# A new order of one instruction list: a state-space scan and a low-rank mixer on one core

## Chip, cores and metric

The kernel runs on one core of a Trainium2 chip. The metric is the device time of one execution in microseconds (us), median of the runs. The engines are TensorE (PE in the profile, PEld for its weight loads), VectorE (DVE), ScalarE (ACT), GpSimd (POOL) and SyncE (SP), whose queue issues all the loads and stores.

## What is computed

The first part is a chunked scan over 4 batches of 8 heads, 768 tokens, 32 channels and 16 states; the second mixes tokens through a rank of 32 and channels through two weight matrices.

```python
# scan: x (4,8,768,32), a (4,8,768), B and C (4,8,768,16); chunks of 32 tokens
cum = cumsum(log(a) in the chunk)
M = (C @ B.T) * exp(cum_i - cum_j) * causal
y = M @ x + (C @ state) * exp(cum)
state = exp(cum_last) * state + sum_j exp(cum_last - cum_j) * B_j x_j
# bridge: (b, h, s, d) -> x (4, 768, 256)
# mixer: U (768,32), V (32,768), w_ch1 (256,1024), w_ch2 (1024,256)
u = x + ((x.T @ U) @ V).T
out = u + relu(u @ w_ch1) @ w_ch2
```

U, V and the two matrices arrive as 64-bit floats. The kernel loads them as 32-bit words and makes fp32 of them itself.

## The kernel before

The scan is cut into 12 pairs of 128-token blocks, three for each batch: pairs 0 to 2 are batch 0, 3 to 5 batch 1, and so on. The mixer works on a batch in two halves of 384 tokens and on the hidden size in eight slices of 128. Batch 0 takes plain fp32 products for its channel mixing; the later batches split each operand into parts of fewer bits (near, far, and a joined one) and multiply those in a faster type.

Nothing is scheduled by the compiler. A string, PLAN, holds some 900 words, and `follow` runs through it, so each engine gets its instructions in the order of the words. A word is a letter and its indices. Each engine runs its own list in order and waits on semaphores for the others, so a word that waits on an engine holds back all the words behind it there. The letters that matter here:

- F n: n fill products are put ahead of the next product that takes a PSUM bank (`idle`, L139). Nobody reads them; one is two records in the profile.
- A 0, A 1: the decay products (L370, L374) and their Exp (L377). K: the decays between chunks (L385 to L397).
- Q k.c and P k: B and C of pair k times their decays, on VectorE (tile BC), in three parts or at once. V k.c.v and T k: transposes of BC (L475) and the copies of them (T, Cm).
- g k: C times B (L507, banks x and z). m k and M k: the causal mask over its first and second half, on VectorE (tile M). s k: what a pair adds to the state (L542), u k: the state itself (tile S on VectorE, Sm on GpSimd).
- n k, i k, j k: the outputs of pair k (L652, L627, L652), in two banks y. j waits for a tiny VectorE copy (tile `settled`) behind n and i. y k: their copies (L670). t k and O k.v: the transposes to token order (L679).
- c n: the next of three steps that make fp32 of a loaded chunk (the generator `to_fp32`): VectorE and ScalarE first, then VectorE, then GpSimd (L422). Chunk 0 is U and V together, 1 and 2 are the halves of the first quarter of w_ch1, 3 to 5 its other quarters, 6 to 9 are w_ch2. v: V spread and split (L838 to L848).
- R n: the next step that splits a converted chunk into its parts (`refine`: ScalarE, then GpSimd at L436, with ScalarE and VectorE).
- p b, q b: the projection by U (L705, L713). a b.j: u of half j (L723 on TensorE, adds on VectorE).
- U 0.j.m: the plain products of slice m for batch 0 (L751, tile w1f) and their Relu. S, f, e, h: the split of u and the first product of the later batches. d: the second product, in pieces, and the output.
- B k, X k, w n, L k: loads of pair k's B and C, of its x, of a weight chunk (w 0 and 1 are halves of 256 KB, the others 512 KB, and chunk number n + 1 is made of w n), and of both B and X. A load word in PLAN carries a wait for the last VectorE instruction ahead of it (`hold`).

All loads go through SP's queue, in order. In the kernel before, the first nine (LOADS: B0 X0 B1 V0 U0 X1 B2 X2 B3) stand ahead of the plan and wait for nothing.

All VectorE rows of the profile have line L169, that of a helper, so one goes by the tiles.

Of the kernel before, what the change touches and what calls it, by code (L numbers as in the profile page):

```python
# [10 lines left out]
FP32 = mybir.dt.float32  # L11
INT32 = mybir.dt.int32
UINT32 = mybir.dt.uint32
FP32R = mybir.dt.float32r
WCOLS = 512
NWORDS = 15
# [14 lines left out]

LOADS = (
    'B0 X0 B1 V0 U0 X1 B2 X2 B3 ')
PLAN = (
    'F5 A0 Q0.0 F1 F2 F4 w0 Q0.1 A1 Q0.2 V0.0.0 Q1.0 V0.1.1 K0 s0 Q1.2 g0 m0 Q1.1 M0 V1.0.2 '
    'V1.1.2 u0 n0 g1 c0 c0 c0 M1 F1 i0 Q2.0 s1 j0 y0 m1 Q2.2 Q2.1 V2.0.2 u1 V2.1.3 n1 i1 g2 j1 y1 '
    'B5 s2 m2 M2 w1 v0 u2 O0.0 w2 w3 c1 c1 c1 i2 P3 n2 j2 y2 t1 X3 T3 T3 B4 c2 c2 P5 O2.1 p0 g3 '
    'c3 c3 w4 w5 m3 q0 M3 T5 w6 T5 a0.1 a0.0 s3 X4 c4 c4 c2 P4 U0.1.0 c5 c3 U0.0.3 U0.0.0 U0.0.2 '  # L40
    'c4 c5 B6 X5 U0.1.1 T4 T4 U0.0.4 u3 n3 c6 i3 R2 g4 s4 j3 R1 M4 R0 c5 X6 m4 u4 U0.0.7 P6 c6 '
    'U0.1.7 w7 U0.0.5 w8 y3 U0.1.6 U0.1.4 R1 s5 n4 i4 c6 g5 c7 c7 c7 L8 u5 j4 y4 T6 T6 U0.0.1 M5 '
    'U0.0.6 m5 c9 n5 i5 R4 g6 c8 c8 j5 y5 t4 d0.1.0.0 t3 m6 t5 U0.1.5 c9 L7 c9 R7 U0.1.2 P8 p1 '
    'U0.1.3 M6 R5 P7 R3 q1 d0.1.0.1 c8 d0.1.0.2 d0.1.0.3 d0.0.1.0 a1.0 R0 S1.0 d0.0.2.0 d0.0.2.1 '
    'd0.0.2.2 d0.0.2.3 L10 T7 d0.0.1.1 d0.0.1.2 R3 T7 d0.0.1.3 n6 R2 R5 g7 m7 s6 f1.0.4 M7 a1.1 '
    'u6 f1.0.1 e1.0.4 h1.0.4 f1.0.0 f1.0.5 e1.0.1 e1.0.0 h1.0.0 d0.0.0.0 e1.0.5 d0.0.0.1 R4 L9 T8 '
    'f1.0.6 h1.0.5 f1.0.7 T8 e1.0.6 d0.0.0.2 h1.0.1 d0.0.0.3 e1.0.7 i6 s7 j6 f1.0.2 d0.1.2.0 R6 '
    'h1.0.6 h1.0.7 y6 f1.0.3 e1.0.2 h1.0.2 d0.1.2.1 u7 e1.0.3 h1.0.3 S1.1 P9 d0.1.2.2 d0.1.1.0 '
    'd0.1.2.3 d0.1.1.1 d0.1.1.2 d0.1.1.3 n7 R4 g8 m8 i7 M8 s8 d1.0.0.0 d1.0.0.1 R6 R7 R7 R6 R5 u8 '
    'f1.1.1 d1.0.0.2 L11 d1.0.0.3 d1.0.1.0 f1.1.0 s9 P10 j7 y7 d1.0.0.4 e1.1.0 u9 h1.1.0 d1.0.0.5 '  # L50
    'd1.0.1.1 e1.1.1 d1.0.1.2 d1.0.2.0 d1.0.2.1 h1.1.1 f1.1.6 d1.0.2.2 f1.1.7 d1.0.1.3 e1.1.6 T9 '
    'h1.1.6 T9 d1.0.1.4 d1.0.1.5 T10 d1.0.2.3 e1.1.7 t7 h1.1.7 f1.1.3 f1.1.2 d1.0.2.4 d1.0.2.5 '
    'e1.1.2 h1.1.2 T10 e1.1.3 f1.1.4 f1.1.5 n8 i8 s10 j8 e1.1.4 e1.1.5 y8 d1.1.0.0 h1.1.3 '
    'd1.1.1.0 d1.1.1.1 h1.1.4 P11 d1.1.0.1 h1.1.5 d1.1.2.0 d1.1.2.1 d1.1.0.2 d1.1.0.3 u10 '
    'd1.1.2.2 d1.1.2.3 d1.1.0.4 d1.1.0.5 d1.1.1.2 d1.1.1.3 d1.1.2.4 d1.1.2.5 d1.1.1.4 d1.1.1.5 t6 '
    't8 g9 m9 p2 T11 i9 M9 q2 T11 g10 m10 n9 M10 a2.0 s11 j9 u11 y9 g11 m11 S2.0 M11 i10 t9 n10 '
    'f2.0.0 f2.0.4 f2.0.5 e2.0.0 j10 h2.0.0 y10 e2.0.4 h2.0.4 f2.0.1 e2.0.5 h2.0.5 f2.0.2 e2.0.1 '
    'h2.0.1 f2.0.6 f2.0.3 e2.0.2 e2.0.6 f2.0.7 h2.0.2 e2.0.3 h2.0.6 i11 n11 j11 h2.0.3 e2.0.7 '
    'd2.0.0.0 h2.0.7 d2.0.1.0 d2.0.1.1 y11 a2.1 S2.1 d2.0.0.1 d2.0.0.2 d2.0.0.3 d2.0.1.2 d2.0.1.3 '
    't10 t11 d2.0.1.4 d2.0.1.5 d2.0.0.4 d2.0.0.5 f2.1.1 f2.1.0 f2.1.2 f2.1.3 e2.1.0 h2.1.0 e2.1.1 '  # L60
    'h2.1.1 p3 e2.1.2 d2.0.2.0 h2.1.2 d2.0.2.1 d2.0.2.2 q3 f2.1.4 e2.1.3 h2.1.3 d2.0.2.3 f2.1.5 '
    'e2.1.4 d2.0.2.4 d2.0.2.5 e2.1.5 f2.1.7 h2.1.4 h2.1.5 f2.1.6 d2.1.2.0 a3.0 e2.1.6 e2.1.7 '
    'd2.1.0.0 h2.1.6 a3.1 d2.1.0.1 d2.1.0.2 d2.1.2.1 d2.1.2.2 S3.0 f3.0.2 f3.0.3 f3.0.4 h2.1.7 '
    'd2.1.0.3 d2.1.2.3 e3.0.2 f3.0.7 h3.0.2 e3.0.3 d2.1.0.4 d2.1.0.5 e3.0.4 f3.0.6 d2.1.1.0 '
    'd2.1.1.1 d2.1.1.2 f3.0.5 h3.0.3 e3.0.6 d2.1.2.4 e3.0.7 h3.0.4 e3.0.5 h3.0.6 h3.0.7 f3.0.0 '
    'd2.1.1.3 h3.0.5 f3.0.1 d2.1.2.5 e3.0.0 e3.0.1 d2.1.1.4 h3.0.0 d2.1.1.5 S3.1 d3.0.2.0 '
    'd3.0.2.1 d3.0.0.0 h3.0.1 d3.0.0.1 f3.1.2 f3.1.3 d3.0.2.2 d3.0.2.3 f3.1.5 f3.1.0 d3.0.2.4 '
    'd3.0.2.5 e3.1.2 h3.1.2 e3.1.3 h3.1.3 d3.0.0.2 d3.0.0.3 d3.0.1.0 f3.1.4 d3.0.1.1 f3.1.1 '
    'e3.1.4 h3.1.4 e3.1.5 h3.1.5 e3.1.0 e3.1.1 h3.1.0 d3.0.1.2 d3.0.1.3 h3.1.1 d3.0.0.4 f3.1.6 '
    'f3.1.7 d3.0.1.4 e3.1.6 d3.0.1.5 e3.1.7 d3.0.0.5 d3.1.2.0 d3.1.2.1 h3.1.6 h3.1.7 d3.1.2.2 '  # L70
    'd3.1.2.3 d3.1.1.0 d3.1.1.1 d3.1.2.4 d3.1.2.5 d3.1.1.2 d3.1.1.3 d3.1.0.0 d3.1.0.1 d3.1.0.2 '
    'd3.1.0.3 d3.1.1.4 d3.1.1.5 d3.1.0.4 d3.1.0.5 ')


@with_exitstack
def kernel(
# [28 lines left out]
    P = 128  # L105
    NB, NH, S, D = x.shape
    N = B.shape[-1]
    NC = S // P
    NPR = NC // 2
    DM = NH * D  # L110
    RK = moe_U.shape[1]
# [6 lines left out]
    NQ = NM // 2  # L118
# [75 lines left out]
    def begin(**kwargs):  # L194
        op = nc.sync.dma_start(**kwargs)
        if until:
            hold(op, until.pop())

    def load_bc(k, blocks=(0, 1)):
        b, q = pairs[k]  # L200
        if k not in bc_sb:
            bc_sb[k] = raw.tile([P, NH, 2, 2, N], FP32, tag="bc", name="bc")
        for c in blocks:
            begin(
                out=bc_sb[k][:, :, 0, c],
                in_=B[b, :, ts(2 * q + c, P), :].rearrange("h s n -> s h n"))
            if c == 0:
                begin(
                    out=bc_sb[k][:, :, 1].rearrange("p h t n -> p h (t n)"),
                    in_=C[b, :, ts(q, 2 * P), :].rearrange("h (p t) n -> p h (t n)", t=2))  # L210
# [17 lines left out]
    w1all = mix.tile([P, NQ, NCB, W], FP32, tag="u", name="w1f", bufs=1)  # L228
    w1f = [w1all[:, c] for c in range(NQ)]
    w2 = [const.tile([P, NM, DM], FP32R, name=f"w2{i}") for i in range(2)]  # L230
    weights = []
    w2f, w2b = {}, {}

    def w2c(n, dtype):
        return (w2f if dtype == FP32 else w2b).setdefault(n, mix.tile(
            [P, 2, DM], dtype, tag=f"w2c{n}", name=f"w2c{n}", bufs=1))


    def words_of(dst):
        p, i, j = dst.shape  # L240
        t = raw.tile([P, 2 * WCOLS], INT32, tag="words", name="words", bufs=NWORDS)
        weights.append((dst, t[:p, :2 * i * j]))
        return t[:p, :2 * i * j]

    def each(parts, *index):
        return [part[index] for part in parts]

    def load_words(dst, src):

        p, i, j = dst.shape  # L250
        t = words_of(dst)
        begin(out=t.rearrange("p (i j) -> p i j", i=i), in_=src)

    U2, V2, w12, w22 = (w.bitcast(INT32) for w in (moe_U, moe_V, moe_w_ch1, moe_w_ch2))
# [3 lines left out]
    own = {}  # L258

    def load_v():  # L260
        own["UV"] = words_of(UV)
        for q in range(4):
            begin(out=own["UV"][ts(q, Q), 2 * NC * RK:], in_=V2[:, ts(q, 2 * NC * RK)])

    def load_u():
        begin(out=own["UV"][:, :2 * NC * RK].rearrange("p (c r) -> p c r", c=NC),
                          in_=U2.rearrange("(c p) r -> p c r", p=P))

    def load_w(n):
        if n < 2:  # L270
            if n == 0:
                own["w"] = words_of(w1f[0])
                weights.pop()
            dst, t = w1f[0][:, :, ts(n, P)], own["w"][:, ts(n, 2 * NCB * P)]
            weights.append((dst, t))
            begin(out=t.rearrange("p (i j) -> p i j", i=NCB),
                  in_=w13[:, :, ts(n, 2 * P)])
        elif n <= NQ:
            load_words(w1f[n - 1], w13[:, :, ts(n - 1, 2 * quarter)])
        else:  # L280
            m = 2 * (n - NQ - 1)
            load_words(w2c(n - NQ - 1, FP32), w22[m * P:(m + 2) * P].rearrange(
                "(m p) d -> p m d", p=P))

    def load(k):
        if k < NB * NPR:
            load_bc(k)
            load_x(k)

    loads = dict(B=load_bc, X=load_x, w=load_w)  # L290
    for word in LOADS.split():
        dict(loads, V=lambda n: load_v(), U=lambda n: load_u())[word[0]](int(word[1:]))

    ident = const.tile([P, P], FP32)
    make_identity(nc, ident)
# [578 lines left out]
    def ytokens_of(k, v):  # L874
# [1 line left out]

    scans = dict(P=prep, T=turned, g=gram, s=state, m=lambda k: mask(k, (0, 1)),
                 M=lambda k: mask(k, (2, 3)), u=update, i=inter, n=lambda k: intra(k, 0),
                 j=crossed, y=yout, t=ytokens, L=load, Q=lambda k, c: prep(k, c, 1),
                 O=ytokens_of,  # L880
                 V=lambda k, c, v: turn(k, c, 1, "wx"[v // 2], vector if v % 2 else None))
    whole = dict(c=convert, R=refined, A=lambda i: decays(every_batch, "w", [i]),
# [3 lines left out]
    def follow(plan):  # L886

        for word in plan.split():
            name, at = word[0], [int(v) for v in word[1:].split(".")]
            if name in "BXwL":  # L890
                until[:] = [vector.last]
            if name in loads:
                loads[name](*at)
            elif name in scans:
                scans[name](*at)
            elif name in whole:
                whole[name](*at)
            else:
                b, *at = at
                if b not in mx:  # L900
                    mx[b] = mixer(b)
                getattr(mx[b], name)(*at)
            until.clear()
# [32 lines left out]
```

## Time and profile before

| | before |
|---|---|
| median of 3 runs | 230.32 us (229.53 to 230.38) |
| the profiled execution | 229.32 us |
| its span | 227.6 us |
| TensorE busy, records | 215.0 us (94%), 3004 |
| VectorE busy, instructions | 146.5 us (64%), 312 |
| ScalarE busy, instructions | 107.9 us (47%), 250 |
| GpSimd busy, instructions | 33.9 us (15%), 43 |
| moved by DMA | 14.56 MB in 69,518 packets, 63,792 of them under 512 B |
| packets that carry instructions | 23 of queue q8 (0.38 MB), 7 of q14 |

An engine's busy time is the sum over its instructions. A matmul's end is modelled, since products overlap in the array, so TensorE busy is not TensorE at its peak. The chain of waits runs back from the last instruction to what released each step; its pieces are given as start, length, engine, tile and line. "issue" is time in which an engine waited for nothing that the profile shows. Windows are stretches of the span, with each engine's busy time and instruction count in them, the granted TensorE clock (PEclk, 1.00 is full), the share of the DMA engines and GB/s.

### The profile page before, as it was taken

The numbers are of one execution on the slowest core, as the hardware profiler recorded it, in microseconds if no ns is written. First come the engines' busy times: TensorE is split into PE (matmuls) and PEld (weight loads), VectorE is DVE, ScalarE is ACT, GpSimd is POOL, SyncE is SP. The second block draws the span as 40 slices with busy tenths as digits, with TensorE's granted clock in tenths as the row PEclk, the third lists the DMA queues.
The fourth block names the chain that finished last, engine by engine and source line by source line (L and its number), as shares of the span: only waits on it lengthen the run. The fifth ranks groups of instructions, "written<-read, shape, count | busy, mean of one in ns | idle before, by whom it ended". The sixth has DMA issues, their size and how long they took to land.

```text
span 227.6 us, 6973 instructions
## 1 busy us (share of the span) xinstructions
PE 215.0 (94%) x3004; PEld 183.3 (81%) x3004; DVE 146.5 (64%) x312; ACT 107.9 (47%) x250; POOL 33.9 (15%) x43
## 2 busy tenths in 40 slices
PE   7867979999999999999999999999999999999993
PEld 5644636666658889887999897698999999999993
DVE  4597867678632686479746546967746964945731
ACT  2334643756854366532456511465445654636410
POOL 3031232335075003015200010000000000000000
PEclk9999988999999999999999999999999999999999
DMA  6896878976560164211430001000010000000011
GB/s 95 137 130 111 154 180 162 232 106 202 80 94 23 35 106 49 42 32 50 53 65 27 22 27 49 3 3 0 3 46 3 24 0 26 23 23 26 23 46 46
DMA packets 69518, 14.56 MB, mean 64 GB/s; under 512 B 63792, under 2 KB 67696, under 8 KB 69488
## 3 DMA queue, kind: packets, MB, share of 16 engines
q1 hardware_dynamic: 69488, 14.13, 31.5%
q8 instruction: 23, 0.38, 0.6%
q14 instruction: 7, 0.06, 0.1%
HBM read 10.98 MB, written 3.15 MB: 62 GB/s over the span
## 4 chain that ended last, share of the span: by engine, by line
PE 82%; DVE 10%; issue 2%; ACT 2%; POOL 1%; POOLq 0%; DVEq 0%
PE x L751 29%; PE z L751 20%; PE y L751 12%; PE y L652 3%; PE y L627 3%; DVE M L169 3%; PE x L507 2%; PE w L679 2%; DVE words L169 2%; PE w L705 2%; DVE S L169 2%; PE w L475 2%; DVE BC L169 2%; PE w L542 1%; PE w L139 1%
## 5 line engine op out<-in xcount | busy, mean ns | idle before, releaser
L751 PE MATMUL x<-u,w 128*128 128x384 f32 x144 | 33.3, 345 | 0.1
L751 PE MATMUL z<-u,w 128*128 128x384 f32 x144 | 33.0, 344 | 0.0
L169 DVE SCALAR_TENSOR_TENSOR words<-words 128x768 fp32r<-128x768 f32 (+3 forms) x34 | 29.7, 873 | 2.1 <-PE y L751 0.4
L751 PEld LDWEIGHTS x<-u,w 128*128 128x128 f32 x144 | 24.5, 188 | 1.1 <-ACT words L785 0.4
L751 PEld LDWEIGHTS z<-u,w 128*128 128x128 f32 x144 | 24.8, 188 | 0.3
L169 DVE SCALAR_TENSOR_TENSOR words<-x,words 128x384 fp32r<-128x384 f32 x24 | 13.2, 555 | 17.7 <-ACT words L785 17.5
L756 ACT ACTIVATE x<-x 128x384 f32<-128x384 f32 (+1 forms) x30 | 13.7, 455 | 21.8 <-PE x L751 19.6
L751 PE MATMUL x<-w2c,words 128*128 128x256 f32 x112 | 22.4, 338 | 0.0
L756 ACT ACTIVATE z<-z 128x384 f32<-128x384 f32 (+1 forms) x27 | 12.5, 464 | 15.3 <-PE z L751 14.4
L569 POOL TENSOR_TENSOR Sm<-S,own 128x256 f32<-128x256 f32 (+1 forms) x12 | 7.7, 640 | 78.6 <-DVE S L169 60.1
L751 PEld LDWEIGHTS x<-w2c,words 128*128 128x128 f32 x112 | 18.3, 189 | 1.4
L751 PE MATMUL y<-w,words 128*128 128x256 f32 x144 | 19.3, 282 | 0.0
L751 PEld LDWEIGHTS y<-w,words 128*128 128x128 f32 x144 | 18.6, 190 | 0.0
L169 DVE SCALAR_TENSOR_TENSOR words<-z,words 128x384 fp32r<-128x384 f32 x24 | 13.2, 552 | 2.6 <-ACT words L785 2.6
L785 ACT ACTIVATE words<-x 128x384 fp32r<-128x384 f32 x24 | 11.7, 493 | 6.8 <-PE x L751 6.8
L785 ACT ACTIVATE words<-z 128x384 fp32r<-128x384 f32 x24 | 11.7, 491 | 6.7 <-PE z L751 6.7
L169 DVE TENSOR_TENSOR BC<-bc,F 128x512 f32<-128x512 f32 (+2 forms) x18 | 10.4, 594 | 5.5 <-ACT F L377 2.8
L507 PE MATMUL x<-Cm,T 32*64 32x128 f32 x192 | 11.0, 306 | 2.5 <-issue 1.4
L652 PE MATMUL y<-M,x 64*32 64x64 f32 x768 | 12.0, 223 | 1.5 <-DVE settled L169 1.5
L751 PE MATMUL x<-w,words 128*128 128x256 f32 x96 | 13.4, 284 | 0.0
L652 PEld LDWEIGHTS y<-M,x 64*32 64x32 f32 x768 | 8.2, 105 | 6.0 <-DVE settled L169 2.7
L751 PEld LDWEIGHTS x<-w,words 128*128 128x128 f32 x96 | 12.6, 190 | 0.1
(148 smaller groups left out, 406.4 us busy)
## 6 DMA issues: line engine op xcount, KB each, us to landing
words<-in_moe_w_ch_dram SPq DMA_DIRECT2D x7, 512.0 KB, 5.6
x<-in_x_dram SPq DMA_DIRECT2D x24, 128.0 KB, 3.4
out_dram<-ytok SPq DMA_DIRECT2D x24, 128.0 KB, 1.7
bc<-in_B_dram SPq DMA_DIRECT2D x24, 64.0 KB, 3.0
bc<-in_C_dram SPq DMA_DIRECT2D x12, 128.0 KB, 3.1
words<-in_moe_w_ch_dram SPq DMA_DIRECT2D x2, 256.0 KB, 3.2
words<-in_moe_V_dram SPq DMA_DIRECT2D x4, 48.0 KB, 2.0
words<-in_moe_U_dram SPq DMA_DIRECT2D x1, 192.0 KB, 3.0
```

Source lines behind the costliest of these rows:

```text
L139: nc.tensor.matmul(out=t[:, :m * w].rearrange("p (m i) -> p m i", i=w), lhsT=ident, rhs=ident[:, None, :w].to_broadcast([P, m, w]), start= ...
L169: self.last = call(*args, **kwargs)
L475: nc.tensor.transpose(out=tp[:, i, v], in_=s["BC"][:, i, c + v].rearrange("p h n -> p (h n)"), identity=ident)
L507: nc.tensor.matmul(out=g[r][cols, c], lhsT=s["T"][rows, 0, c, cols], rhs=s["Cm"][rows, :, :, ts(2 * c + p, Q)].rearrange("r v t i -> r v i ...
L569: nc.gpsimd.tensor_tensor(out=s["Sm"][:, sl], in0=s["S"][:, sl].rearrange("p i (s d) -> p i s d", s=2), in1=own2[:, b, 4 * q + sl.start:4 ...
L627: behind["first"].append(nc.tensor.matmul(out=y[r // 2][ts(r % 2, H), c, p], lhsT=own[ts(r, Q)], rhs=s["T"][ts(r, Q), 1, :, ts(2 * c + p, ...
L652: product = nc.tensor.matmul(out=y[n][ts(i, Q), c, p], lhsT=x_sb[k][half, c, h], rhs=s["M"][half, h // 2, c, h % 2], start=fresh(k, n, [i] ...
L679: nc.tensor.transpose(out=t[:, c, g], in_=yT[b][:, g, ts(2 * q + c, P)], identity=ident)
L705: nc.tensor.matmul(out=p[ts(c % 4, Q)], lhsT=U_sb[:, c], rhs=ytok[b][:, c], start=c < 4, stop=True, skip_group_check=True)
L751: nc.tensor.matmul(out=t, lhsT=lhsT, rhs=rhs, start=start, stop=True, skip_group_check=True)
L756: nc.scalar.activation(t, t, AF.Copy, scale=1.0 + EPS)
L785: nc.scalar.activation(gs[j, m // 2][0][:, m % 2], t, AF.Relu, scale=NEAR)
```

## The change

The operations stay as they are. PLAN is replaced by another order of the same words, from its first word to its last, and the load words are mixed into it:

- F5 and the last of F1 F2 F4 ahead of A0 and A1, and an F1 later (ten fills), become F2 ahead of A0 and F2 ahead of V0.0.0 (four fills).
- The first nine loads become words with a Y ahead of their letter (YB0, YX1, YV0). They wait for nothing, as before. Their order is now B0 B1 X0 X1 V0 B2 U0, then w1, which waits, then X2 and B3: V and U come behind the second x.
- The three steps of c0 go from behind g1 to places among the words of pairs 1 and 2, right ahead of v0.
- The chunks of w_ch1 are loaded in the order w1 w2 w0 w4 w3 w5 instead of w0 w1 w2 w3 w4 w5, and converted in an order to match, with the first steps of c2 and c3 between the words of pairs 2 and 3 and c1 behind a0 and a1. The U products start with slices 3, 2, 1, 0 instead of 0, 3, 0, 2.
- n3 goes ahead of the first U. The later scans, splits and products have another order too.
- L goes; B and X are separate words for all pairs.

The head of the plan, before and after (the rest of the list is left out; it is reordered in the same way):

```diff
-LOADS = (
-    'B0 X0 B1 V0 U0 X1 B2 X2 B3 ')
 PLAN = (
-    'F5 A0 Q0.0 F1 F2 F4 w0 Q0.1 A1 Q0.2 V0.0.0 Q1.0 V0.1.1 K0 s0 Q1.2 g0 m0 Q1.1 M0 V1.0.2 '
-    'V1.1.2 u0 n0 g1 c0 c0 c0 M1 F1 i0 Q2.0 s1 j0 y0 m1 Q2.2 Q2.1 V2.0.2 u1 V2.1.3 n1 i1 g2 j1 y1 '
-    'B5 s2 m2 M2 w1 v0 u2 O0.0 w2 w3 c1 c1 c1 i2 P3 n2 j2 y2 t1 X3 T3 T3 B4 c2 c2 P5 O2.1 p0 g3 '
-    'c3 c3 w4 w5 m3 q0 M3 T5 w6 T5 a0.1 a0.0 s3 X4 c4 c4 c2 P4 U0.1.0 c5 c3 U0.0.3 U0.0.0 U0.0.2 '
-    'c4 c5 B6 X5 U0.1.1 T4 T4 U0.0.4 u3 n3 c6 i3 R2 g4 s4 j3 R1 M4 R0 c5 X6 m4 u4 U0.0.7 P6 c6 '
-    'U0.1.7 w7 U0.0.5 w8 y3 U0.1.6 U0.1.4 R1 s5 n4 i4 c6 g5 c7 c7 c7 L8 u5 j4 y4 T6 T6 U0.0.1 M5 '
-    'U0.0.6 m5 c9 n5 i5 R4 g6 c8 c8 j5 y5 t4 d0.1.0.0 t3 m6 t5 U0.1.5 c9 L7 c9 R7 U0.1.2 P8 p1 '
-    'U0.1.3 M6 R5 P7 R3 q1 d0.1.0.1 c8 d0.1.0.2 d0.1.0.3 d0.0.1.0 a1.0 R0 S1.0 d0.0.2.0 d0.0.2.1 '
+    'YB0 F2 A0 Q0.0 A1 YB1 Q0.1 F2 Q0.2 V0.0.0 Q1.0 YX0 V0.1.1 K0 g0 Q1.2 m0 Q1.1 M0 s0 V1.0.2 '
+    'V1.1.2 YX1 YV0 n0 g1 u0 i0 YB2 Q2.0 s1 m1 YU0 j0 y0 w1 Q2.2 M1 Q2.1 YX2 n1 u1 V2.0.2 V2.1.3 c0 '
+    'i1 YB3 g2 c0 B5 w2 j1 X3 M2 w0 B4 y1 s2 m2 c0 v0 O0.0 t1 u2 i2 n2 c2 j2 y2 P3 T3 T3 P5 O2.1 c3 '
+    'w4 c3 p0 c3 g3 m3 q0 T5 T5 M3 a0.0 c2 a0.1 c1 n3 w3 s3 U0.0.3 U0.0.2 X4 c2 P4 U0.0.1 T4 T4 w5 '
+    'c1 c1 U0.1.0 u3 i3 U0.1.1 c5 c5 X5 w7 j3 y3 c4 c4 R0 g4 c4 s4 m4 M4 B6 w8 w6 X8 U0.1.2 U0.0.0 '
+    'u4 i4 g5 n4 s5 j4 m5 c5 R3 B7 U0.0.4 U0.0.5 B8 X6 B11 y4 M5 R0 c6 X10 u5 U0.1.4 t3 c8 c8 R1 c6 '
+    't4 U0.0.7 P6 T6 T6 U0.0.6 R3 U0.1.3 c8 R6 U0.1.7 c6 c9 n5 i5 g6 j5 y5 B9 d0.0.2.0 m6 M6 c9 c9 '
+    't5 U0.1.5 c7 c7 c7 P7 U0.1.6 p1 d0.1.0.0 R1 T7 X7 R2 T7 q1 d0.0.1.0 R2 d0.0.2.1 d0.0.2.2 '
...
```

The code around it: the loaded chunks are kept by number instead of in the order of loading, V and U may come in either order, and `follow` knows the Y words.

```diff
-    weights = []
+    weights = {}
...
-    def words_of(dst):
+    def words_of(c, dst):
...
-        weights.append((dst, t[:p, :2 * i * j]))
+        weights[c] = dst, t[:p, :2 * i * j]
...
+    def both_words():
+        return weights[0][1] if 0 in weights else words_of(0, UV)
...
-    for word in LOADS.split():
-        dict(loads, V=lambda n: load_v(), U=lambda n: load_u())[word[0]](int(word[1:]))
+    early = dict(loads, V=lambda n: load_v(), U=lambda n: load_u())
...
-            name, at = word[0], [int(v) for v in word[1:].split(".")]
-            if name in "BXwL":
+            name, rest = (word[:2], word[2:]) if word[0] == "Y" else (word[0], word[1:])
+            at = [int(v) for v in rest.split(".")]
+            if name in "BXw":
                 until[:] = [vector.last]
-            if name in loads:
+            if name[0] == "Y":
+                early[name[1]](*at)
+            elif name in loads:
                 loads[name](*at)
```

## The prediction

> **What bounds the kernel now.** I read the page's slices first, then the stretches by window, then the chain of waits where TensorE is not full. In the slices below (5.7 us a digit) PE is TensorE's busy share, PEclk its granted clock, DMA the share of the transfer engines.
>
> ```profile
> PE   7867979999999999999999999999999999999993
> PEclk9999988999999999999999999999999999999999
> DMA  6896878976560164211430001000010000000011
> ```
>
> TensorE is full from the seventh slice on; the first six are not, and there the DMA engines are nearly full. The windows put numbers on it.
>
> ```profile
> core 0: us, PE busy (x) PEld busy (x) DVE busy (x) ACT busy (x) POOL busy (x), PEclk, DMA share, GB/s
> 0.00:34.00 34.00, 26.13 (x617) 18.04 (x617) 23.49 (x73) 14.65 (x42) 8.01 (x20) 0.98 0.78 135
> 34.00:56.00 22.00, 21.83 (x375) 13.84 (x383) 16.51 (x39) 12.74 (x27) 8.15 (x7) 0.95 0.78 178
> 56.00:105.00 49.00, 48.42 (x592) 39.50 (x582) 30.16 (x61) 26.02 (x56) 14.47 (x13) 1.00 0.36 56
> 105.00:224.00 119.00, 118.43 (x1442) 111.92 (x1442) 75.96 (x141) 54.54 (x126) 3.29 (x5) 1.00 0.10 26
> ```
>
> From 34 us to 224 us TensorE has 1.3 us free in 190 us. What it has to do there is the same list before and after, so a new order can gain only in the first 34 us, of which TensorE is busy 26, and can lose anywhere. The mark between the two is the word a0.1 (with a0.0: the first products of L723, at 33.96 us): ahead of it all three scans of batch 0, behind it the stream of U, f, e and d products. How early the marks come is what I work out. The head's chain begins so:
>
> ```profile
> 3.50 0.48 PE x L139 x2
> 3.98 1.89 PE w L139 x10
> 5.86 0.33 PE w L370 x2
> 6.19 0.89 PE w L139 x8
> 7.08 0.53 PE w L374 x8
> 7.63 0.35 ACT F L377
> 8.00 0.44 DVE BC L169
> ```
>
> The fill products (L139), whose results nobody reads, stand on the chain. The Ln of the decays ends at 4.43 us (ScalarE's timeline), but A0 (L370) waits until 5.70 behind ten fill records, and A1 (L374) behind eight more. Every later step of the first scan hangs on A1's F, through Q0.2 at 8.00. Next VectorE, where word c0 (conversion of V and U) stands between two masks:
>
> ```profile
> 14.12 1.05 DVE L169 TENSOR_SCALAR words<-words 128x384 f32<-128x384 f32 x2
> 15.21 0.56 DVE L169 SCALAR_TENSOR_TENSOR words<-words 128x384 int32<-128x384 int32 x1
> 15.69 0.75 DVE L169 TENSOR_TENSOR M<-z,causal 128x256 int32<-128x256 int32 x2
> ```
>
> The second mask waits out the conversion, and both conversion rows are on the chain of waits. Last, the end of the head:
>
> ```profile
> 29.37:32.78 3.41, 2.02 (x37) 1.12 (x35) 2.46 (x5) 1.18 (x3) 1.61 (x2) 1.00 0.77 182
> 32.78:36.19 3.41, 3.34 (x41) 2.20 (x39) 2.69 (x8) 2.27 (x5) 0.41 (x1) 0.50 0.64 80
> ```
>
> In the first stretch TensorE stands for 1.39 us at 30.46 in the middle of g3, with no releaser in the profile ("issue"). In the same two microseconds the DMA engines are at 97.8% with data and one 16 KB instruction packet passes. In the second stretch the granted clock is half.
>
> **The change part by part.** The sum is made against the profiled execution (229.32 us; span 227.6, and 1.7 around it). The median of the runs is 230.32, 1.00 above it; I move that median by the sum.
>
> *Fills.* F5 ahead of A0 becomes F2: six records fewer at 0.21, so A0 starts at about 4.62 (just after the Ln) instead of 5.70. The clock is still low there, A0 costs 0.33 more, and F of A0 comes 0.75 earlier. A1 follows it directly, without eight records (0.89 on the chain): F of A1 starts at about 6.0 instead of 7.63. The F2 that is left stands ahead of V0.0.0, while VectorE forms Q0.1 and Q0.2, and costs nothing; uncovered it is 0.44. -1.6 (bounds -1.2, if that cover fails, and -1.6). C0's load, issued at 1.74 and 2.9 us to landing, is there at 4.6.
>
> *Conversions ahead of a0.* Before has c0 whole, c1 whole, two steps of c2 and two of c3; after has c0 whole, one step of c2, c3 whole. On VectorE a half chunk costs 0.29+0.45 and then 0.42, a full one 0.46+0.48 and then 0.75. That is 1.16+1.16+1.69 before and 0.74+1.69 after: 1.6 us less, c0 alike. VectorE is busy 13.3 of the 16 us from 8 to 24, and such rows are on the chain, so I take all of it: -1.6 (bounds 0, if they fall into its waits, and -1.6).
>
> *The 1.39 us in g3.* Before, three weight loads (256, 512 and 512 KB) are issued from 23.7 to 24.9, and the 512 KB ones need 5.6 us and more to land. After, only w2 of these is issued close ahead of g3 (w0 is a half, w4 and w3 come later). If the stop is an instruction packet behind data, it shrinks; if not, it stays. -0.9 (0 to -1.4), nearer to the gain because one large load instead of two lies ahead. The Trainium skill (Runtime: NRT & Kernel Launch, "Instruction fetch mechanics") says that blocks of 16 KiB are fetched while the one before runs, mostly hidden; by that rule this term would be 0, and the idle 1.39 beside the packet speaks against it.
>
> *Half clock.* 3.41 us at half speed come after a stretch with 2.02 us busy of 3.41; the least busy stretch of that length ahead of it that kept its clock has 2.33 (19.13 to 22.54). After has fewer fills but denser work. -0.3 (bounds +1.0 for one such stretch more, as a third of 3.41 lay on the chain, and -1.0).
>
> *V and U.* V's four loads go behind X1, U's behind B2. Nobody reads them before c0, which goes from behind g1 to behind V2.1.3, past u0, m1, M1, u1 and Q2 on VectorE (some 5 us by their rows), so the later landing is free; without that cover it would be X1's and B2's issue time, 4.3 us. But c0's last step (1.01 on GpSimd) now stands shortly ahead of v0, where TensorE waited 0.8 for Vn already. y1, M2 and m2 cover most of it: +0.2 (0 to +0.7).
>
> *Loads with a wait.* w1's load now waits for VectorE's copy ("settled") of j0; behind it on SP's queue are X2 and B3, which waited for nothing before. That copy moves up with the scan, from 16.98 to about 14, X2 was issued at 14.06, and s2 and P3 need them at about 20 and 24: nothing, and up to +1.0 if the copy is late.
>
> *Behind a0.* n3 goes ahead of the first U, 0.4 there and back. The U products now go chunk 1, chunk 0, then 2 and 3, which gives w3 and w4 longer to be converted. Against it, R0, u5, c6, c8 and P6 stand in a row on VectorE while TensorE does two t and four U: c6, c8 and P6 4.2, u5 0.9, R0 1.0 to 1.8, some 7.5, against 0.9+5.2 on TensorE from U0.0.5 on. VectorE is about a microsecond late at T6, less what the waits there cost before: +0.6 (0 to +2.9). The late order (105 to 224): TensorE had 0.6 idle, 0 (-0.6 to +1.0).
>
> Sum: -1.6 -1.6 -0.9 -0.3 +0.2 +0.6 = -3.6 us. That is 225.7 for the profiled execution and **226.7 for the median**.
>
> **The rivals.** *VectorE becomes the bound between a0 and q1 (slower).* Counted from the rows, the words from a0.0 to q1 give VectorE 28.3 us (six full conversions 10.1, twelve mask products 5.0, three R 3.0, eleven S updates 3.1, P 2.4, a 2.2, the rest 2.5) and TensorE 33.9 (sixteen U 20.6). VectorE runs in order. Let each R wait as the worst one before (1.16 for GpSimd, and 1.76 long instead of 0.99), add all load waits of before (2.9) and one settled wait in each of three scans (1.36): 41.1, 7.2 more than TensorE. In place of my +0.6 that gives 233.3. It decides from 4.2 us on. For it: after starts this stretch earlier with more left to convert. Against it: the chunks are asked for later.
>
> *Loads set the start (no change).* The DMA share is 0.78 over the head. If U0.0.3 waits for w2 or T5 for B5 in spite of the new order, only the 0.9 of the stop is won: 229.4. For it: w2's hold on c0's second step. Against it: w2 was issued at 24.4; its hold stands beside g2, which ran at 20.6 and moves up with the scan.
>
> *The clock drops twice.* Fewer fills could leave two stretches of the head under the bar, somewhere from 2.02 to 2.33 busy, instead of one: 1.0 each and the -0.3 gone, 229.0. For it: from 12.3 to 22.5 us before had 2.3 to 2.5 a stretch. Against it: the waits between its products get shorter. The Trainium skill (TensorE: Matmul & The Clock Gate, "What's actually happening") gives half clock after an idle window of about 3.4 us; by that rule no stretch here would drop, and the drop after 2.02 busy disagrees.
>
> **How the numbers follow.** About 0.5% (1.15 us) is what can be told from no change: faster means under 229.2, slower over 231.5. My forecast has 0.60, VectorE bound 0.20, loads 0.11, clock 0.09. Forecast and clock give faster 0.69; loads 0.11 no change; VectorE 0.20 slower. The forecast's own range is 224.3 to 229.2 (all gains at their ends but one, or P6 at +2.9). The range reaches to 232.0, most of the way into the VectorE case, and leaves out under 2 in 10.
>
> **What would show it.** In the profile after: A0 at 4.6 and Q0.2 at 6.4; c0's rows no longer between the masks of pair 1; the first L723 product near 30; no idle of over 1 us in g3; no half clock from 32.8; from there to the end some 190 us as before. I am wrong if L723 comes at 33 or later (loads, or VectorE's sum in the head), or if it comes at 30 and TensorE then shows over 3 us of new waits for VectorE's BC, words or masks between 30 and 70.

## The result, and the profile after

The changed kernel takes 231.55 us (median of 20 runs, 229.25 to 232.95) against 230.20 for the kernel before beside it (20 runs, 228.46 to 231.73). The ratio is 1.0046, interval 1.0023 to 1.0068: 0.46% slower, at the edge of the 0.5% that the prediction took for no change, where 226.7 us and faster was forecast. The profiled execution has 231.93 us, span 230.2. Lines move up in the new file, those of the products by six and VectorE's helper by two: L723 of before is L717, L751 is L745, L652 is L646, L507 is L501, L475 is L469, and L169 is L167. (PLAN has 556 words before and 567 after, not some 900 as was said above.)

The slices of the page, TensorE's busy share, its granted clock and the transfer engines' share:

```profile
PE   7967889999999999999999999999599999999994
PEclk9995699999999999999999999999999999999998
DMA  6978873989981150021300001000010001000011
```

Two things are new: a clock of 0.5 to 0.6 in the fourth and fifth slice (17 to 28 us), and a 5 in the 29th slice of PE (161 to 167 us). The same windows as before:

```profile
core 0: us, PE busy (x) PEld busy (x) DVE busy (x) ACT busy (x) POOL busy (x), PEclk, DMA share, GB/s
0.00:34.00 34.00, 27.73 (x603) 18.57 (x603) 21.41 (x69) 15.10 (x42) 6.41 (x18) 0.85 0.81 134
34.00:56.00 22.00, 21.91 (x393) 13.97 (x394) 16.36 (x44) 11.20 (x27) 8.38 (x9) 1.00 0.78 183
56.00:105.00 49.00, 48.09 (x545) 38.59 (x544) 31.29 (x60) 26.87 (x60) 14.05 (x13) 1.00 0.40 62
105.00:224.00 119.00, 116.47 (x1430) 109.13 (x1429) 77.02 (x140) 54.65 (x124) 4.20 (x5) 1.00 0.08 23
```

From 34 to 224 us TensorE now has 3.5 us free (190 less 186.47), where it had 1.3. And the head gave nothing: the first L717 product starts at 33.90, where L723 started at 33.96. So the 4.2 us that the terms of the head were to bring did not come, and some 3 us were lost late (from the start of the first U product to that of TensorE's last product it takes 190.8 us after and 187.7 before).

**The late loss** shows in TensorE's waits from 105 to 224 us (line waited for: us in total, times, longest), first after, then before:

```profile
PE y L646 <- DVE settled L167: 2.5, 1, 2.5
```

```profile
PE x L507 <- DVE ytok L169: 0.5, 1, 0.5
PE y L652 <- DVE settled L169: 0.3, 1, 0.3
PE x L723 <- DVE M L169: 0.2, 1, 0.2
PE z L723 <- DVE M L169: 0.2, 1, 0.2
```

The engine timelines after (start, length, line, tiles; in brackets the idle time and who ended it) show the place, j11, the second part of the last pair. VectorE's rows, then TensorE's:

```profile
163.51 0.96 DVE L167 TENSOR_TENSOR u<-yT,u 128x768 fp32r<-128x768 f32 x1 [0.97 <-ACT u L740]
164.50 0.96 DVE L167 SCALAR_TENSOR_TENSOR u<-u 128x768 fp32r<-128x768 f32 x1
165.38 0.15 DVE L167 COPY settled<-x 128x1 f32<-128x1 f32 x1
```

```profile
162.68 0.39 PE L583 MATMUL x<-ident 128*128 128x128 f32 x2
165.58 0.46 PE L646 MATMUL y<-M,x 64*32 64x64 f32 x32 [2.52 <-DVE settled L167]
```

The word j11 issues a product (L583), a copy of it on VectorE (settled), and then the 32 products that wait for that copy. In the new order a2.1 and S2.1 come ahead of j11, so the copy stands behind S2.1's two splits of 0.96, and the first of those waits for ScalarE. In before j11 came ahead of them. The other late stop is T6. The row below names ScalarE, but T6 transposes BC of P6, and that is ready only at 57.88:

```profile
55.88 1.46 PE L745 MATMUL z<-yT,w1f 128*128 128x384 f32 x4
58.03 0.63 PE L469 MATMUL w<-ident,BC 128*128 128x128 f32 x4 [0.70 <-ACT w L426]
```

**The head** begins as forecast. A0 starts at 4.60, Q0.2 at 6.75 (8.00 before), the first mask at 10.09 (11.41), j0's settled copy at 14.43 (16.98): 2.55 us ahead. At j1's copy 1.44 us of that are left (19.55 against 20.99), and at j1's products nothing (21.56 against 21.39). From j0's copy to j1's products lie the first of three windows at half clock, and two stops of TensorE that the profile ascribes to no releaser:

```profile
15.35 0.46 PE L646 MATMUL y<-M,x 64*32 64x64 f32 x31 [0.47 <-issue]
...
20.95 0.58 PE L501 MATMUL z<-Cm,T 32*64 32x128 f32 x3 [0.62 <-issue]
```

```profile
13.94:17.36 3.42, 2.41 (x123) 1.78 (x116) 2.51 (x10) 0.65 (x2) 0.00 (x0) 1.00 0.72 163
...
17.36:20.77 3.41, 2.60 (x63) 1.70 (x62) 2.27 (x8) 1.74 (x5) 1.62 (x2) 0.50 0.81 118
20.77:24.19 3.42, 2.63 (x92) 1.62 (x91) 2.26 (x8) 0.90 (x3) 0.00 (x0) 0.50 0.87 99
24.19:27.60 3.41, 3.41 (x72) 2.61 (x56) 1.01 (x3) 2.49 (x7) 0.51 (x1) 0.50 0.86 202
```

Counted in TensorE's own instructions (weight loads, products, semaphores), the stops fall at number 449 and 705, and that of before in g3 at 1217: each is 193 and a multiple of 256. Such a number is called a boundary here. A packet of queue q8 carries 16 KB, and there is one for each boundary: I read from the times that it is asked for about when TensorE gets to a boundary, and that it brings the 256 instructions behind the *next* one. In the stretch after the 449th instruction (14.66 us) the queues hold, first until 18.7 and then until 19.7:

```profile
q1 hardware_dynamic: 3418, 0.74, 90.0%
```

```profile
q1 hardware_dynamic: 1303, 0.12, 95.0%
q8 instruction: 1, 0.02, 5.8%
```

Four us pass with 0.74 MB of data (w1, x, B, C) before the packet starts at 18.75; it ends at 19.68, and TensorE, at the 705th instruction since 19.92, goes on at 20.95.

### The profile page after: what moved, and what is told of

The parts are those of the page before. It is cut to its first block, busy times and chain, and to the rows that moved or that the text cites. A ratio compares the mean times of both kernels' runs of the same rounds, so it can differ in the third digit from the quotient of the medians.

```text
span 230.2 us, 6952 instructions
## 1 busy us (share of the span) xinstructions
PE 217.1 (94%) x2990; PEld 183.0 (79%) x2990; DVE 146.9 (64%) x312; ACT 108.2 (47%) x250; POOL 33.1 (14%) x43
## 4 chain that ended last, share of the span: by engine, by line
PE 85%; DVE 6%; ACT 3%; DMA 3%; issue 1%; POOL 1%; SPq 0%; POOLq 0%; ACTq 0%
PE x L745 29%; PE z L745 22%; PE y L745 12%; PE y L646 3%; PE y L621 3%; DMA x<-in_x_dram 3%; PE x L501 2%; PE w L469 2%; PE w L699 2%; DVE words L167 1%; PE w L536 1%; PE w L673 1%; PE z L501 1%; PE w L707 1%; PE x L137 1%
## 5 line engine op out<-in xcount | busy, mean ns | idle before, releaser
L745 PE MATMUL z<-u,w 128*128 128x384 f32 x144 | 33.2, 346 | 0.0
L745 PE MATMUL x<-u,w 128*128 128x384 f32 x144 | 33.0, 344 | 0.0
L167 DVE SCALAR_TENSOR_TENSOR words<-words 128x768 fp32r<-128x768 f32 (+3 forms) x34 | 30.2, 890 | 1.8
L745 PEld LDWEIGHTS z<-u,w 128*128 128x128 f32 x144 | 24.4, 188 | 0.9 <-DVE M L167 0.2
L745 PEld LDWEIGHTS x<-u,w 128*128 128x128 f32 x144 | 24.5, 188 | 0.6
L745 PE MATMUL x<-w2c,words 128*128 128x256 f32 x112 | 22.3, 340 | 0.2 <-DVE M L167 0.2
L167 DVE SCALAR_TENSOR_TENSOR words<-x,words 128x384 fp32r<-128x384 f32 x24 | 13.2, 553 | 12.1 <-ACT words L779 11.9
L745 PE MATMUL y<-w,words 128*128 128x256 f32 x144 | 19.8, 283 | 0.0
L745 PEld LDWEIGHTS x<-w2c,words 128*128 128x128 f32 x112 | 17.9, 189 | 2.1 <-ACT words L762 0.4
L745 PEld LDWEIGHTS y<-w,words 128*128 128x128 f32 x144 | 18.9, 190 | 0.1
L167 DVE SCALAR_TENSOR_TENSOR words<-z,words 128x384 fp32r<-128x384 f32 x24 | 13.3, 553 | 7.9 <-ACT words L779 7.9
L750 ACT ACTIVATE z<-z 128x384 f32<-128x384 f32 (+1 forms) x27 | 12.6, 467 | 12.1 <-PE z L745 11.6
L646 PE MATMUL y<-M,x 64*32 64x64 f32 x768 | 12.2, 227 | 3.9 <-DVE settled L167 2.9
L646 PEld LDWEIGHTS y<-M,x 64*32 64x32 f32 x768 | 8.0, 108 | 8.7 <-DVE settled L167 3.5
L745 PE MATMUL x<-w,words 128*128 128x256 f32 x96 | 14.2, 287 | 0.0
L664 ACT COPY yT<-y 128x256 f32<-128x256 f32 x24 | 7.8, 380 | 13.5 <-PE y L646 13.5
L167 DVE SCALAR_TENSOR_TENSOR S<-S,kept,w 128x64 f32<-128x64 f32 x40 | 11.2, 279 | 3.8 <-PE w L536 2.1
L745 PEld LDWEIGHTS x<-w,words 128*128 128x128 f32 x96 | 12.8, 190 | 0.7 <-issue 0.4
```

The costliest lines, as they stand in the source:

```text
L167: self.last = call(*args, **kwargs)
L646: product = nc.tensor.matmul(out=y[n][ts(i, Q), c, p], lhsT=x_sb[k][half, c, h], rhs=s["M"][half, h // 2, c, h % 2], start=fresh(k, n, [i] ...
L664: nc.scalar.copy(out=yT[b][:, n, ts(q, 2 * P)], in_=st[k]["y"][n].rearrange("p c v i -> p (c v i)"))
L745: nc.tensor.matmul(out=t, lhsT=lhsT, rhs=rhs, start=start, stop=True, skip_group_check=True)
L750: nc.scalar.activation(t, t, AF.Copy, scale=1.0 + EPS)
```

## The experiments

Four theories were put on the chip. *Late order*: j11's wait is the late loss. *P6*: T6's wait is. *Clock*: fewer fills let the clock fall. *Loads and supply*: what lies ahead in the transfer queues, B2 or the instruction packet, takes back the early start. Ratios are to the kernel before, run beside each (its median was 229.6 to 230.42). A gap that is given without a row, here and in the expectations, runs from the start of the last product to the start of the next one. The idle time in a row leaves out that last product's own modelled length, and is 0.2 to 0.5 us shorter.

**a_settle: j11 back ahead of the splits.**

```diff
-d2.0.0.2 a2.1 S2.1 d2.0.1.1 d2.0.1.2 d2.0.0.3 j11 y11 d2.0.1.3
+d2.0.0.2 j11 y11 a2.1 S2.1 d2.0.1.1 d2.0.1.2 d2.0.0.3 d2.0.1.3
```

> The new order with j11 y11 moved back ahead of a2.1 S2.1; all else as in the new order. Theory 1 (the late order costs what the trace shows): TensorE's 2.5 us wait for the settled copy behind S2.1 goes, and nothing else comes late; 231.55 - 2.4 = about 229.1. Theory 2 (VectorE is late there anyway, and the wait only moves to the next f or h): 231.5, with a new wait of about 2 us between 163 and 175 us.

229.82 us, ratio 0.9975 (0.9937 to 1.0013). j11's gap falls from 2.79 to 0.73 us (in the rows from 2.52 to 0.46 idle). The one edit takes 0.7% off the changed kernel, and the two intervals do not meet: the late order is one cause.

**a_p6: P6 ahead of the conversions.**

```diff
-t3 c8 c8 R1 c6 t4 U0.0.7 P6 T6 T6
+t3 P6 c8 c8 R1 c6 t4 U0.0.7 T6 T6
```

> The new order with P6 moved ahead of the two steps of c8 and of c6 on VectorE. Theory 1: T6 no longer waits (1.0 us between two L469 and L745 products near 57 us) and the time falls by about 0.9, to 230.6. Theory 2 (VectorE is the bound of this stretch): the wait comes back within 10 us at another VectorE result, and the time stays at 231.5.

230.16 us, ratio 1.0021 (0.9986 to 1.0055). T6's wait is gone from TensorE's waits, so it was P6; j11's gap is still there (2.81 at 159.90), with two half windows behind it in the profile (162.2 to 169.0). That is 0.25% off, and the intervals overlap: the time alone does not show this gain.

**a_fills: nine fill words more in the head.**

```diff
-n0 g1 ... Q2.0 s1 ... u1 V2.0.2 ... y1 s2
+n0 F4 g1 ... Q2.0 F2 s1 ... u1 F2 V2.0.2 ... y1 F1 s2
```

> The new order with nine more fills in the head: four ahead of g1, two ahead of s1, two ahead of V2.0.2, one ahead of s2. Theory 1 (the half clock from 17.4 to 27.6 us took the head's gain): granted clock full up to 31 us, the first product of a0.0 at about 31.5 instead of 33.9, time about 229.3. Theory 2 (the stops of TensorE without a releaser and the loads hold the head): the clock is full and a0.0 still comes at 33 or later, time 231 to 232, with stops still where TensorE's instruction count is 193 + 256 n (these runs: 449, 705, 1217).

234.17 us, ratio 1.0174 (1.0125 to 1.0223), over 2 us above what either theory had. The profile has full clock in the whole head and the first a0 product at 32.23, but TensorE has a gap of 1.51 at 49.20 (1.29 idle in its row), half clock follows from 51.1 to 54.5, and again from 167.1 to 170.5 behind j11's stop. The 24 instructions more move the words under the boundaries: the stops are in g3 (a gap of 0.98 at number 1217) and in the scan at 49.20 (number 1985). The fills mend the clock and break the supply.

**b_head: the kernel before with the new order's fills ahead of V0.0.0 (its later F1 stays).**

```diff
-F5 A0 Q0.0 F1 F2 F4 w0 Q0.1 A1 Q0.2 V0.0.0
+F2 A0 Q0.0 w0 A1 Q0.1 F2 Q0.2 V0.0.0
```

> The kernel before with only its first words changed: two fills ahead of A0, none ahead of A1, two ahead of V0.0.0, as in the new order. My first term alone: F of A1 1.6 us earlier and all of it kept up to a0.1, so 230.2 - 1.6 = 228.6. Rival (loads, instruction supply and clock decide the head, so an early start is given back before a0.1): first L723 product within 0.4 us of 33.96, time 230.2.

229.00 us, ratio 0.9979 (0.9951 to 1.0008). The scan is 1.2 us ahead as far as g2 (i1 at 19.06 against 20.28), then VectorE waits 2.50 for the load of w1 (0.56 before), issued 0.26 us earlier than before (23.45) and landed at 27.68, and the first a0 product comes at 34.08 (33.96 before). The start is really earlier, and it is given back by a0: the wait for the load takes most of it. The profile also has half clock from 13.1 to 16.5 and from 30.2 to 33.6, so the load's share alone is not settled.

**a_both: j11 and P6 together.**

> The kernel after with j11 y11 ahead of a2.1 S2.1 and P6 ahead of c8 c8 R1 c6 (both edits that were run alone). If the late loss of after is those two waits (2.8 at j11's L646, 1.18 at T6) and they stand in different places of the same full TensorE, their gains add: 1.7 and 1.2 us under after, about 228.6 us, ratio to before 0.993, U to the last product about 188. If one of the two measured gains was only the luck of the clock's windows, it comes out like j11's edit alone: 229.8, ratio 0.998.

228.08 us (226.59 to 230.16), ratio 0.9912 (0.9880 to 0.9943): faster than both kernels, and 1.3% below the changed one. In TensorE's waits from 105 us on there is left (the profile is of its slowest run, 230.16):

```profile
PE y L646 <- DVE settled L167: 0.4, 1, 0.4
PE z L745 <- DVE u L167: 0.4, 1, 0.4
```

From the first U to the last product it takes 188.65 us (187.66 before). So these two words are 2.1 of the 3.1 us that were lost there. The 1.0 us that is left is not idle time (1.1 us idle in this stretch, 1.3 before); what takes it stays open. What the runs differ by is in the head: four runs have a mean granted clock of 0.999 or more and take 226.6 to 227.4 us, five have 0.977 or 0.978 and take 228.4 to 230.2. That is full clock against three half windows of 3.41 us, and with the stops that go with them they are worth 2.4 us between the two middles.

**b_settle: the mirror, j11 behind the splits in the kernel before.**

> The kernel before with the opposite edit: j11 y11 behind a2.1 S2.1 as in after, no other change. Theory (VectorE's place): the copy named settled waits behind the two splits of S2.1, j11's L646 stands some 2 us more, 232.2 to 232.7 us, ratio 1.009 to 1.011, or 1.7 more where half clock follows the stop. Rival (before's order has VectorE free by then): the wait stays near the 0.7 it has now and the time is that of before.

232.94 us, ratio 1.0118 (1.0080 to 1.0157). VectorE's rows of the kernel before with that one edit:

```profile
163.89 0.96 DVE L169 TENSOR_TENSOR u<-yT,u 128x768 fp32r<-128x768 f32 x1 [0.97 <-ACT u L746]
164.88 0.96 DVE L169 SCALAR_TENSOR_TENSOR u<-u 128x768 fp32r<-128x768 f32 x1
165.76 0.15 DVE L169 COPY settled<-x 128x1 f32<-128x1 f32 x1
```

These are the same three rows as after. j11 waits 2.8, and a half window follows at 166.7 (the profile is of the slowest run). The cause holds in both directions.

**a_light: a_both with F2 ahead of g1, F1 ahead of s1, F2 ahead of n1 (12 instructions).**

> As a_both, with three fill words more in the scans of pairs 1 and 2: F2 ahead of g1, F1 ahead of s1, F2 ahead of n1 (12 instructions of TensorE instead of the 24 of the nine fills, so that boundary 1985 of its instructions stays among the U products). Theory (clock): two of the three half windows of the head go, first a product near 31 instead of 32 to 33, no stop of over 1 us at 1985 and no half clock near 51, time 1 to 1.5 us under a_both: 227.3, ratio 0.987. Rival (loads and supply set the head): the clock is kept but the first a product stays within 0.5 us, and the time is that of a_both. Rival (fills too few): half clock from 17 as before, time that of a_both or up to 0.4 above.

228.04 us, ratio 0.9916 (0.9897 to 0.9935): the time of a_both, with a spread of 1.1 us instead of 3.6. The clock is full through the head and the first a0 product comes at 31.40. But there is a gap of 1.3 us at the 1985th instruction, which I had expected to be gone: the block from 1729 on now takes 3.1 us, and its packet ran only from 48.42 to 49.37. (The row puts its 0.83 idle down to VectorE's S, which ends at 51.06, so the packet is not the only candidate here.) What matters is how long after its packet TensorE comes to a boundary, not which word lies under it.

**a_zero: a_both with F1 for F2 ahead of A0, F2 ahead of g1 and n1; a_w1: a_both with w1 behind X2 and B3; a_zero_w1: both.**

```diff
-YU0 j0 y0 w1 Q2.2 M1 Q2.1 YX2 n1 u1 V2.0.2 V2.1.3 c0 i1 YB3 g2
+YU0 j0 y0 Q2.2 M1 Q2.1 YX2 n1 u1 V2.0.2 V2.1.3 c0 i1 YB3 w1 g2
```

> a_both with the fills moved: F1 instead of F2 ahead of A0, and F2 ahead of g1 and F2 ahead of n1 (four instructions of TensorE more than a_both, where the run with three fill words more had twelve). Theory (fills keep the clock, but every instruction that they add brings the 1985th closer to the 1729th): full clock in the head as in the run with three words more, the first a product within 0.3 us of its 31.4, and the stop of 1.3 us at 1985 down to 0.5 or less: 227.2, ratio 0.9875, with a spread of under 1.5 us instead of 3.6. Rival (four instructions are too few, or F1 lets the clock fall early): half clock from 7 or from 17 in the profile, a spread like that of a_both and its median, 228.1.

> a_both with the load word w1 (256 KB) moved from behind y0 to behind the load words X2 and B3, so that it is issued some 4 us later. Theory (instruction packet behind data): in a_both and in after the second packet of 16 KB, asked for when TensorE passes its 449th instruction at 14.6, starts only at 18.8 to 19.1 behind w1, x and B, and TensorE stands 1.0 to 1.65 us at the 705th instruction until 1.3 to 1.6 us after the packet's end. With w1 out of the way the packet starts about 1.3 us earlier and that stop falls under 0.5 us; the first a product 1 us earlier, time 0.5 us under a_both (227.5, ratio 0.989). Rival (the stop has another cause): the stop at 705 stays over 0.9 and the time is that of a_both, or worse where c2 now waits for w1.

> Both edits together: the fills as in a_zero, w1 as in a_w1. If clock and instruction supply are two causes that each cost the head, the gains add up: first a product near 31, 226.6, ratio 0.985, near the time that was predicted for the changed kernel. If the loads set the head once the clock is kept, it is a_zero's time within 0.3 us.

a_zero 228.30 us, ratio 0.9910 (0.9874 to 0.9945), and a_zero_w1 227.62, 0.9896 (0.9864 to 0.9928), both 1 us over what was expected; a_w1 226.67, 0.9863 (0.9828 to 0.9899, four runs), 0.8 us under it. The one fill less ahead of A0 costs a_zero the start. In its profile TensorE's products run at about half pace beyond 9 us:

```profile
8.21 0.85 PE L379 MATMUL z<-la,middle 128*128 128x192 f32 x2
8.85 0.74 PE L382 MATMUL z<-la,high 128*128 128x160 f32 x2
```

(0.49 and 0.43 in the profile after), and the 193rd instruction comes at 12.0 instead of 10.2. The trace records the first grant of full clock at 10.72 us, and at 7.12 after; the windows count the time ahead of that record as full clock. In a_w1 the packet that is asked for at 14.09 starts at 16.98, the gap at 705 is 0.75 (0.46 idle), and the first a0 product comes at 30.59.

**after_w1: the changed kernel with w1's edit alone; a_best: a_w1 with F2 ahead of n1.**

> The kernel after with the load word w1 behind X2 and B3 and nothing else changed (the late order and P6 as in after). Theory (three separate losses: j11's wait 1.7, P6 1.2, w1 ahead of the instruction packet 1.4): only the last is undone, 230.1 us, ratio 0.999; the stop at 705 under 0.8, j11's stop of 2.8 still there. Rival (w1's edit won only by the clock's luck in four runs): 231.3, ratio 1.004, and the stop at 705 stays at 1.0.

> The three edits together (j11 ahead of the splits, P6 ahead of c8, w1 behind X2 and B3) with one F2 ahead of n1, where TensorE waits 0.5 for yT anyway; F2 stays ahead of A0, so the first stretches are as dense as in after. Theory: full clock in the head in the profile and in nearly all runs, four instructions more, no stop of over 0.5 at 1985: 226.6 us, ratio 0.985, spread under 1.5 us. Rival (the clock of the head hangs on more than one fill): the median is that of the three edits without the fill, 226.7 to 227.5, with runs up to 229.

after_w1 231.41 us, ratio 1.0042 (1.0018 to 1.0066), where I expected 230.1; a_best 228.84, 0.9912 (0.9879 to 0.9945), where I expected 226.6. Both miss, and their two profiles show one reason. From VectorE's waits from 8 to 34 us in after_w1:

```profile
DVE BC L167 <- DMA bc<-in_B_dram: 2.1, 1, 2.1
```

In a_best that wait is 2.3. V's four transfers stand ahead of B2 on SP's queue. In both profiles B2's first part lands at 15.1, in a_w1's at 12.6, and VectorE asks for it at 12.3 to 13.1, so there is no slack. Issued at 10.48 in after it landed at 12.77; issued at 10.91 in a_best it landed at 15.14. What stands ahead of B2 on the queue is the same in after, a_w1 and these two, so it is the execution that decides, and one profile does not tell how many runs were late.

**a_v: a_both with V behind B2; a_v_w1: a_w1 with V behind B2; a_v_w1_f: that with F2 ahead of n1.**

```diff
-YX1 YV0 n0 g1 u0 i0 YB2 Q2.0 s1 m1 YU0 j0
+YX1 n0 g1 u0 i0 YB2 Q2.0 s1 m1 YV0 YU0 j0
```

> a_both (j11 ahead of the splits, P6 ahead of c8) with V's load word moved from ahead of B2 to behind it, so that B2's three transfers are issued 1.9 us earlier. Theory (B2 set the head): with V's four transfers ahead of it, B2's first part lands at 12.5 to 12.8 with VectorE asking for it at 12.8 to 13.1 (no slack), at 15.1 in two runs, and the part of C at 14.4 to 15.3 with VectorE waiting 0.4 to 0.7. Moved, VectorE waits for neither, the settled copy of j0 comes at 13.9 or earlier in every profile and the time falls by 0.7 where B2 was in time and by 2.5 where it was late: median 227.2, ratio 0.988. Rival (clock and instruction packet set the head): the wait for C goes, but the stop at 705 and the half windows stay, 228.1, as a_both.

> As a_v, with w1 behind X2 and B3 as well (the edit that gave 226.7 in four runs with B2 in time, and nothing in a kernel whose profile has B2 2.1 us late). Theory (B2 late is what took that gain away): B2 is in time in every run and the four runs' time is met by all: 226.3 to 226.8, ratio 0.983. Rival (that time was the clock's luck): median over 227.5 and half windows in the profile.

> As a_v_w1 with F2 ahead of n1. Theory: where all waits for loads are gone, the fill keeps the clock in the rest of the runs: 226.3, ratio 0.982, spread under 1.5 us. Rival (once the loads are in time the stretches are dense enough without it): the time of a_v_w1 within 0.3 us, or 0.2 to 0.4 longer for the fill.

a_v 228.28 us, ratio 0.9907 (0.9871 to 0.9943); a_v_w1 226.75, 0.9874 (0.9830 to 0.9917); a_v_w1_f 226.86, 0.9885 (0.9831 to 0.9938). In none of the three profiles does VectorE wait for B2 (in the last it waits 1.4 for w1, at 23.77, and 1.7 for the next pair's B, at 26.97), but a_v alone gains nothing, as the rival had it: TensorE now only comes sooner to the 705th instruction. The stop there among its waits, then the row of a_v_w1:

```profile
PE z L501 <- issue: 1.6, 1, 1.6
```

```profile
19.08 0.49 PE L501 MATMUL z<-Cm,T 32*64 32x128 f32 x4 [0.33 <-issue]
```

In a_v the packet asked for at 14.40 starts at 18.09, and the gap runs from 18.46 to 20.40 (1.65 idle). With w1 out of its way the packet starts at 16.68, and the gap is 0.62 (18.46 to 19.08, 0.33 idle). The windows that follow, a_v and then a_v_w1:

```profile
17.36:20.77 3.41, 1.65 (x56) 1.17 (x56) 1.25 (x5) 1.00 (x3) 1.06 (x2) 1.00 0.67 95
20.77:24.19 3.42, 2.68 (x93) 1.64 (x92) 3.21 (x10) 1.34 (x6) 0.51 (x1) 0.79 0.76 93
```

```profile
17.36:20.77 3.41, 2.41 (x112) 1.72 (x112) 2.48 (x9) 1.70 (x6) 1.14 (x2) 1.00 0.84 149
20.77:24.19 3.42, 3.14 (x104) 2.18 (x104) 2.05 (x7) 2.30 (x8) 0.51 (x1) 1.00 0.72 105
```

The long stop is followed by a half window (22.7 to 26.2); the short one is not. The first a0 product comes at 32.79 in a_v and at 30.08 in a_v_w1. The fill of a_v_w1_f adds nothing to that. That the two medians differ through w1 is likely, not settled: they were run side by side, but their intervals overlap. a_v_w1, a_w1 and a_v_w1_f are the fastest of all, 1.2 to 1.4% below the kernel before.

## Why the prediction was wrong, point by point

The forecast of 226.7 is about the time of a_v_w1 (226.75), which has the changed plan but for the places of j11 with y11, P6, w1 and V. On the scale of the first comparison its ratio is 227.3 us (226.3 to 228.3). So a gain of that size was there to be had, though in part by another way: a_v_w1's first a0 product comes 3.9 us ahead of before's, where the head's terms had 4.2, and one gain in it, c0's new place, was in no term. Two steps of the sum failed in the changed kernel. Late, a term was put at nothing; in the head, the start was to be kept up to a0, and instruction supply, clock and B2's load took it back.

- **The late order, "0 (-0.6 to +1.0)": wrong.** This term was read from how little TensorE had been idle before, not from the words. The new list moves j11 behind S2.1, and walking it along VectorE's queue gives two splits of 0.96 ahead of the copy, the first of them behind ScalarE. It measured 2.5 at the wait, 0.7% (1.6 us) in a_settle, and +1.2% in b_settle.
- **P6 into T6, +0.6 (0 to +2.9): right.** A gap of 1.18, 0.70 of it idle, that goes with P6's place; 0.25% (0.6 us) in a_p6, which is within its interval. Together with j11 it is 1.3% (a_both against the changed kernel), some 3.1 us. As 0.6 of them were in the forecast, the late words make some 2.5 of the 4.85 us between forecast and result, and the rest is left to the head.
- **Fills, -1.6: right in place, given back.** A0 at 4.60 as said, Q0.2 at 6.75 for 6.4, because the clock was not yet full for A1 either (0.92 instead of 0.57; the trace records full clock from 7.12). At Q0.2 1.25 us are gained, at the first mask 1.3: inside the bounds.
- **Conversions, -1.6: not seen in after.** Up to 34 us VectorE is 2.1 us less busy (21.41 against 23.49), but a0 comes no earlier. What did show is c0's new place, which the sum took as alike: its rows are no longer between the masks of pair 1, and from the first mask to j0's copy the lead grows from 1.3 to 2.55.
- **The stop in g3, -0.9: the cause was right, the conclusion wrong.** It is an instruction packet behind data. But the stop is not tied to g3's loads: a denser scan meets the same limit at 449 and 705, with w1 and pair 3's loads ahead of the packet, in gaps of 0.7 and 1.0 (0.47 and 0.62 idle). The term should have been a bound on the whole head: 256 instructions per packet.
- **Half clock, -0.3 (-1.0 to +1.0): wrong in sign.** Three windows instead of one, in a place that the third rival had in view. The bar I set, between 2.02 and 2.33 busy in 3.41, does not exist: after lost its clock after 2.41, a_w1 kept it through stretches of that length with 2.40 and 2.39, and after itself kept it late, at j11's stop, through 2.34 and 1.97 (160.72 to 167.55).
- **V and U, +0.2 (0 to +0.7): incomplete.** I asked who reads V, and not what stands behind V. B2 does, at the time it always had, while the scan that asks for it came 2.5 us earlier: the wait for C was 0.7 in after, that for B2 2.1 to 2.3 in two experiments. This is the second rival's mechanism, with another load than I named.
- **w1's wait, 0 to +1.0:** harmless for X2 and B3 as said; what it delays is the packet, which was not in the list of what is queued.
- **The first rival, VectorE as the bound from a0 to q1: not seen.** From 34 to 56 us TensorE has 0.1 free (0.2 before), and from there to q1 T6 is the only wait of over 0.2. Its sign came true by another road: VectorE in order, but at one word near the end.

My own test, that I am wrong if L723 (now L717) comes at 33 or later, was met (33.90), with the loads as the reading for it; the runs add supply and clock, and the late word that the test did not cover.

## What to carry to other kernels

When a hand-written order changes as a whole, walk every word that makes TensorE wait for another engine along that engine's new queue, to the very end of the list; an idle sum of the old order says nothing of it. A head that is made denser meets limits that were slack: ask for each load and for the next instruction packet what they land behind, at the new time of need. And an early gain counts only at the mark where the long stream starts.

## What the runs showed of the hardware that was not expected

**Instruction packets.** In nine of the 17 kernels TensorE stopped for 0.3 us or more at instruction 193 + 256k in the head and the scans behind it, and went on 1.27 to 1.50 us after the end of the 16 KB packet that belongs to the boundary ahead of it (1.64 in a_light, where VectorE's S may have a share). Packet and restart were, before: 29.59 to 30.55, on at 31.85; after: 18.75 to 19.68, on at 20.95; a_both: 19.14 to 20.07, 21.52; a_fills: 48.20 to 49.31, 50.70; a_v_w1: 16.68 to 17.61, 19.08. At these stops the packet had started 1.0 to 4.5 us after the boundary, and it took 0.9 to 1.6. An estimate from these figures: where the packet starts no sooner than 1 us after the boundary, a block of 256 instructions that is through in under some 3.2 us stops TensorE. The packet can also start ahead of the boundary, by up to 42 instructions in these 17 traces; in a stretch of long products that is enough. In before the packet of boundary 1729 ran at 50.10, 3.5 us ahead of it, and the 256 instructions behind it went through in 2.31 us without a stop. The Trainium skill (Runtime: NRT & Kernel Launch, "Instruction fetch mechanics") has blocks of 16 KiB fetched ahead and the cost mostly hidden. The block size agrees, and most boundaries here show no stop; at those named the hiding does not hold.

**The clock.** It fell after windows of 3.41 us with as little as 0.76 and as much as 2.70 us busy (b_settle, from 163.31 and from 16.54), and held through others with 1.93 (a_zero, from 27.79), 1.97 (after, from 164.13) and 2.22 (a_w1, from 18.62). So TensorE's busy time, as the profile models it, does not tell which windows cost the clock. It also fell after single gaps of 1.5 to 3.1 us in a full stream (a_fills at 51.1, b_settle at 166.7, a_v at 22.7). It stayed down for one to four windows, and not in every run of the same kernel: j11's stop of 2.5 us was followed by half clock in a_fills, a_p6 and after_w1, and not in after. The Trainium skill (TensorE: Matmul & The Clock Gate, "What's actually happening") has half clock after an idle window of about 3.4 us; no window ahead of these drops was idle throughout.
